# Smaller loads, a split last group on a mixed tile, late tiles inverted first, and a planner with other prices

## The chip, the cores and the metric

The kernel runs on one core of a Trainium2 chip. Its engines are TensorE (PE, with PEld for its weight loads), VectorE (DVE), ScalarE (ACT), GpSimd (POOL, which here issues the gathers) and SyncE (SP, which issues all other transfers). 16 DMA engines move data between HBM and the on-chip memory SBUF; matmuls write into PSUM. The metric is the device time of one execution in microseconds (us).

## The reference

Two branches work on the same x (2048 rows of 576) and are mixed by a gate per row.

```python
def _A_ref(x, w_r, w_i):
    X = rfft2(x)
    return irfft2(X * (w_r + 1j * w_i))

def _B_ref(xf, w_q, k1, k2, u, v):            # 32 heads, K = 1, 64 x 64 experts
    q = einsum("nd,dhc->nhc", xf, w_q)         # 2 x 128 per head
    s1, s2 = q[..., :128] @ k1.T, q[..., 128:] @ k2.T
    e = argmax(s1) * 64 + argmax(s2)           # one expert per row and head
    act = gelu(einsum("nd,nhd->nh", xf, u[e]))
    return einsum("nh,nhd->nd", g * act, v[e]) # g: softmax over one candidate

g = sigmoid((x * gate_w).sum(-1))
return g * _A_ref(x) + (1 - g) * _B_ref(x)
```

## The kernel before

The 2048 rows are 16 tiles of 128. Heads come in 8 chunks `c` of 4. Four kinds of work share the engines.

- **Scores** (`load_wq`, `load_x`, `build_m`, `scores`). For each chunk the weights are multiplied with the keys (`build_m`), five slices `i` of the 576 inputs, of 128 rows each; the fifth holds the last 64 inputs twice. Each operand is split into a high and a low part (`mh`, `ml`, and `xts` for x), and `scores` sums 14 matmuls of 512 columns per tile and chunk. DVE finds the maxima, ACT and DVE turn them into an index (`ei`).
- **Gathers** (`group`). For a tile and a chunk POOL issues four indirect DMAs; each brings, for every one of 128 rows, the 1152 numbers of `u` and `v` of its expert (4608 bytes) into a buffer of the ring `uv` (12 buffers, and one more, `uv2`, late). DVE takes the dot product with x (L496, `z`), ACT the gelu (L500, `b`), DVE the product with the softmax weight (L501, `a`). Then the `v` rows are summed, either by DVE in four multiply-adds (L514) or, where `is_d` holds, on PE: ACT makes diagonal matrices (L524, `dg`) and PE adds eight matmuls into PSUM (`pd`), from which the sum is copied (L538) or added (L540). Of the late tiles 10 to 15, the even ones go by PE, over all eight chunks in one PSUM buffer (`sums`).
- **The transform** (`fold`, `unit` with `f2`, `f4`, `f5`, `f6`): forward along the columns, along the rows, product with the filter, and back along the rows, in ten units.
- **Inversion** (`invert`, `mix`): back along the columns for each tile, with the gate as a scale (L830, L831), then one DVE step (L835) that adds (1 - gate) times the gathered sum, and the store.

Tiles 0 to 9 (`E_T`) have their gathers beside the scores. Then the pools are switched (`switch`), and tiles 10 to 15 (`L_SEQ`) have theirs beside the transform and the inversion, in pairs (10, 11), (12, 13), (14, 15), by `SEQ`.

The order on each engine is not written by hand. Every step is entered in a `Plan` with an engine, an expected duration, a due time `at`, what it reads and writes, and the buffers it needs. `Plan.order` plays the steps through and, whenever an engine is free, takes the one with the smallest due time among those that are ready and find a buffer; the order in which they start there is the order in the program, on SP and POOL too. A gather is entered with 1.13 for its issue and 1.65 for its move. Due times of late groups are spaced `TGS` = 6.6 apart and begin `TLAG` = 10 after the end of the scores, `T0`; those of the transform and the inversion are scaled by `FPACE`, a unit being 14 of it. A due time is no start time: work can be ahead of it or behind it.

PSUM is a ring (`p2`) of four buffers of 128 x 2 x 512, which all matmuls share.

Of the kernel before, what the change touches and what calls it, by code (L numbers as in the profile page):

```python
# [32 lines left out]
def _tables():  # L33
# [10 lines left out]
    def rows(fn, ds):  # L44
        return fn(2 * np.pi * np.outer(ds, k) / D)

    z = np.zeros((P, DF))
    ct = z.copy()
# [4 lines left out]
    fwd = np.stack([  # L53
        rows(np.cos, np.arange(0, 128)), rows(np.cos, np.arange(128, 256)), ct,
        -rows(np.sin, np.arange(0, 128)), -rows(np.sin, np.arange(128, 256)), -st,
    ])
    ck = np.full(DF, 2.0)
    ck[0] = ck[-1] = 1.0
    ck /= S * D

    def irows(fn, ks):
        return fn(2 * np.pi * np.outer(ks, k) / D) * ck[ks][:, None]

    ct = z.copy()
    ct[:33] = irows(np.cos, np.arange(256, 289))
    st = z.copy()
    st[64:96] = irows(np.sin, np.arange(256, 288))
    inv = np.stack([
        irows(np.cos, np.arange(0, 128)), irows(np.cos, np.arange(128, 256)), ct,
        irows(np.sin, np.arange(0, 128)), irows(np.sin, np.arange(128, 256)), st,  # L70
# [12 lines left out]
        "t_fi": c(np.concatenate([fwd, inv]).transpose(1, 0, 2)),  # L83
        "t_f4": c(f4),
        "t_f6": c(f6),
# [167 lines left out]
def tile_kernel(ctx, tc, xn, xT, wqT, kT, wri, uv, gw, t_kr, t_fi, t_f4, t_f6, t_io, out):  # L253
# [84 lines left out]
    gate = pp.tile([P, NT], F32, tag="gate", name="gate")  # L338
    gone = pp.tile([P, NT], F32, tag="gone", name="gone")
# [590 lines left out]
```

## Time and profile before

| | |
|---|---|
| median of 3 runs | 1009.44 us (1008.35 to 1010.46) |
| the profiled execution | 1001.24 us, span 999.5 us |
| mean granted clock of TensorE | 0.965 |
| DVE, PE, DMA queues 0 and 1 | 92%, 90%, 80.9% and 12.3% |
| gathers | 512, 302 MB of 348 MB moved |

Lines of the page and of the trace read as engine, line of the kernel, operation, written tile <- read tiles, shapes, count; a bracket gives the idle time of the engine just before and what ended it. L313 is the line of the helper through which all matmuls go, so matmuls are told apart by their tiles. A busy PE is not a PE at its peak, since the ends of matmuls are modelled.

### The profile page before, as it was taken

How to read it: one execution, taken by the hardware profiler on the slowest of the kernel's cores; microseconds unless marked ns; L12 is line 12 of the kernel's file. 1: busy time of each engine (PE TensorE's matmuls, PEld its weight loads, DVE VectorE, ACT ScalarE, POOL GpSimd, SP SyncE). 2: the span in 40 equal slices, each digit the busy share in tenths (PEclk: the TensorE clock that was granted, in tenths of full speed). 3: DMA queues.
4: the chain of work that ended last, by engine and by line, in shares of the span. 5: the costliest groups of instructions: out<-in, count | busy, mean ns of one | idle time of the engine just before them, and what ended most of it. 6: DMA issues, size and time to landing. Idle time of an engine off the chain costs nothing. (4 is left out here: it accounts for less than half of the span.)

```text
span 999.5 us, 14406 instructions
## 1 busy us (share of the span) xinstructions
PE 904.4 (90%) x4208; PEld 735.8 (74%) x4208; DVE 916.7 (92%) x2255; ACT 514.6 (51%) x1877; POOL 574.4 (57%) x516
## 2 busy tenths in 40 slices
PE   8997999999999999999998990777999998899993
PEld 7885888878877888887877880665777776677762
DVE  3996999999999999999999999999999999977776
ACT  3874676676666576676666664522212222233331
POOL 0354656565656565755657566476655565676662
PEclk9997999999999999999999996889999999899998
DMA  9987999998989999998999799889999999999994
GB/s 336 336 286 301 349 361 367 358 352 305 392 309 361 371 344 332 395 345 328 386 360 330 291 394 378 340 312 389 394 357 351 357 353 321 349 390 414 398 359 192
DMA packets 93246, 348.39 MB, mean 349 GB/s; under 512 B 10480, under 2 KB 13296, under 8 KB 93168
## 3 DMA queue, kind: packets, MB, share of 16 engines
q0 software_dynamic: 73728, 302.02, 80.9%
q1 hardware_dynamic: 19440, 45.45, 12.3%
q8 instruction: 34, 0.56, 0.2%
q14 instruction: 44, 0.36, 0.1%
HBM read 342.71 MB, written 4.72 MB: 348 GB/s over the span
## 5 line engine op out<-in xcount | busy, mean ns | idle before, releaser
L487 POOL DMA_INDIRECT uv<-uv,ei x512 | 574.2, 1121 | 406.2 <-PE p L313 133.3
L313 PE MATMUL p<-mh,xt 128*128 128x512 f32 x1152 | 383.3, 402 | 9.1 <-ACT sg L435 7.3
L435 ACT ACTIVATE sg<-p,mx 128x64 bf16<-128x64 f32 x1024 | 225.8, 352 | 78.1 <-DVE mx L427 55.7
L514 DVE SCALAR_TENSOR_TENSOR xn<-uv,a,xn 128x576 f32<-128x576 f32 x322 | 262.0, 814 | 1.5
L313 PEld LDWEIGHTS p<-mh,xt 128*128 128x128 f32 x1152 | 218.4, 190 | 59.5 <-ACT sg L435 7.7
L313 PE MATMUL p<-ml,xt 128*128 128x512 f32 x640 | 253.2, 396 | 0.0
L496 DVE SCALAR_TENSOR_TENSOR uv<-uv,xn 128x576 f32<-128x576 f32 x320 | 236.3, 749 | 8.7 <-DMA uv<-uv,ei 6.8
L313 PE MATMUL p<-uv,dg 128*128 128x288 f32 x720 | 194.0, 425 | 29.3 <-ACT dg L524 22.5
L313 PEld LDWEIGHTS p<-uv,dg 128*128 128x128 f32 x720 | 140.8, 199 | 77.9 <-ACT dg L524 29.3
L496 DVE SCALAR_TENSOR_TENSOR uv<-uv,xl 128x576 f32<-128x576 f32 x192 | 141.5, 751 | 0.2
L313 PEld LDWEIGHTS p<-ml,xt 128*128 128x128 f32 x640 | 121.6, 190 | 26.6
L500 ACT ACTIVATE b<-z 128x4 f32<-128x4 f32 x128 | 26.4, 206 | 204.9 <-DVE uv L496 171.4
L313 PE MATMUL p<-fi,bt 128*128 128x289 f32 x384 | 97.7, 408 | 4.4 <-DVE t L710 3.0
L313 PEld LDWEIGHTS p<-fi,bt 128*128 128x128 f32 x384 | 83.5, 242 | 16.5 <-issue 3.7
L313 PEld LDWEIGHTS p<-kT,uv 128*128 128x128 f32 x640 | 77.8, 195 | 7.9 <-issue 4.8
L313 PE MATMUL p<-kT,uv 128*128 128x128 f32 x640 | 78.5, 279 | 5.0 <-DMA uv<-wqT 5.0
L427 DVE TENSOR_REDUCE mx<-p 128x16 f32<-128x1024 f32 x64 | 77.5, 1211 | 3.2 <-PE p L313 3.0
L313 PE MATMUL p<-t,t 128*128 128x289 f32 (+2 forms) x384 | 73.8, 362 | 5.9 <-issue 3.4
L446 ACT ACTIVATE sg<-sg 128x256 bf16<-128x256 bf16 x192 | 72.3, 427 | 1.2
L313 PEld LDWEIGHTS p<-t,t 128*128 128x128 f32 (+1 forms) x384 | 54.1, 165 | 23.9 <-issue 10.7
L524 ACT ACTIVATE dg<-ident,a 128x128 f32<-128x128 f32 x180 | 57.6, 393 | 17.7 <-DVE a L501 14.8
L313 PE MATMUL p<-kr,f 128*128 128x128 f32 x160 | 23.0, 301 | 31.5 <-ACT f L648 26.8
(86 smaller groups left out, 612.1 us busy)
## 6 DMA issues: line engine op xcount, KB each, us to landing
uv<-wqT SPq DMA_DIRECT2D x40, 512.0 KB
uv<-uv,ei POOLq DMA_INDIRECT x512
uv<-xT SPq DMA_DIRECT2D x20, 256.0 KB
w<-wri SPq DMA_DIRECT2D x16, 289.0 KB
out<-xn SPq DMA_DIRECT2D x16, 288.0 KB
xn<-xn SPq DMA_DIRECT2D x10, 288.0 KB
t<-t_f SPq DMA_DIRECT2D x18, 128.0 KB
fi<-t_fi SPq DMA_DIRECT2D x2, 867.0 KB
```

Source lines behind the costliest of these rows:

```text
L313: after("PE", nc.tensor.matmul(*args, **kw))
L427: dv(dve(1024, True), at, lambda: nc.vector.tensor_reduce(mv.ap[:, 2 * tp : 2 * tp + 2, :], ps.ap.rearrange("p a (g e) -> p a g e", e=E), ...
L435: on("ACT", actv(sg.ap[:, j, g, :], ps.ap[:, j, g * E : g * E + E], AF.Sign, bias=mv.ap[:, 2 * tp + j, g : g + 1], scale=-1.0))
L446: ac(act(256), at, lambda b=b: actv(s2()[:, :, b * Q : b * Q + Q], s2()[:, :, b * Q : b * Q + Q], AF.Copy, bias=b / 4), [sg], [])
L487: on("POOL", nc.gpsimd.indirect_dma_start(out=g.ap.rearrange("p a d -> p (a d)"), out_offset=None, in_=uv, in_offset=bass.IndirectOffsetOn ...
L496: dv(0.68, at, lambda k=k, g=rows[k]: stt(g.ap[:, 0, :], g.ap[:, 0, :], 1.0, x.ap, op0=ALU.mult, op1=ALU.mult, accum_out=z.ap[:, k : k + 1 ...
L500: ac(0.18, at - 9, lambda: actv(b.ap, z.ap, AF.Gelu_apprx_tanh), [b], zk, table="gelu")
L514: dv(0.73, at, lambda v=v, s=s: stt(y.ap, v(), s(), y.ap, op0=ALU.mult, op1=ALU.add), [y], [(rows[k], 1), a])
L524: ac(0.3, at - 9, lambda k=k, dg=dg: actv(dg.ap, ident, AF.Copy, scale=a.ap[:, k : k + 1]), [dg], [a, "ident"])
```

## The change

- The fifth slice of x and of the weights is loaded once, with 64 rows or columns, instead of doubled (`x5`, `wq5`); the second half of the high part is made on chip, by a second ACT copy in `build_m`. The low part of the fifth slice has 64 rows in its matmul.
- x for blocks 2 and 3 comes in one load for both.
- The inversion uses the same cosine and sine tables (`fi`) as the forward transform; what differed goes into signs, into the fold (a scale of 2 on one column) and into the gate (`gsc`). The two twiddle tables of a unit come in one load (`tw`).
- The place that the second table held goes to a second late gather buffer (`NG2` = 2).
- Late even tiles keep their gathered sum in PSUM until `mix`, which reads it there and writes into the inverted tile; L538 is not used for them. `mix` and the store (`send`) are entered apart.
- Tiles 10 to 15 are inverted first, tiles 0 to 9 after them (`INV`). `FPACE` is 1.4 instead of 1.7.
- The last group (tile 15, chunk 7) is entered in two pairs of gathers, after the tile has been mixed; (1 - gate) is then part of its weights.
- The planner enters a gather with 1.3 for the issue and 1.55 for the move.

```diff
+    fi = np.stack([
+        c0, rows(np.cos, np.arange(128, 256)), ct,
+        rows(np.sin, np.arange(0, 128)), rows(np.sin, np.arange(128, 256)), st,
     ])
...
+        "t_fi": c(fi.transpose(1, 0, 2)),
+        "t_tw": c(np.concatenate([f4[:, :, ::-1], f6], 2)),
...
-        w = wq_t[c, i] = buf("uv", ROW, view=lambda x: x.rearrange("p a d -> p (a d)")[:, : 8 * P].rearrange("p (g e) -> p g e", g=8))
-        ld(load(P * 4096, 4096), at, lambda: nc.sync.dma_start(w.ap, wqT[c, i]), [w], after=after)
-
-    def load_x(b, i, at, at2):
-        st = buf("uv", ROW, view=lambda x: x[:, 0, :512])
-        ld(load(P * 2048, 2048), at, lambda: nc.sync.dma_start(st.ap, xT[:, i, b * 512 : b * 512 + 512]), [st])
-        hi = xts[i if i < 4 else 8][b]
-        lo, r = (xts[4 + i][b], 0) if i < 4 else (hi, 64)
-        ac(act(512), at2, lambda: actv(hi.ap, st.ap, AF.Copy), [hi], [st])
-        dv(dve(512), at2, lambda: vt(lo.ap[r:], st.ap[r:], hi.ap[r:].bitcast(F32), ALU.subtract), [lo], [st, hi])
+        e = P if i < 4 else E
+        w = wq_t[c, i] = buf("uv", ROW, view=lambda x: x.rearrange("p a d -> p (a d)")[:, : 8 * e].rearrange("p (g e) -> p g e", g=8))
+        ld(load(P * e * 32, e * 32), at, lambda: nc.sync.dma_start(w.ap, wqT[c, i] if i < 4 else wq5[c]), [w], after=after)
+
+    def load_x(b, i, at, at2, n=1):
+        st = buf("uv", ROW, view=lambda x: x.rearrange("p a d -> p (a d)")[:, : n * 512])
+        h = P if i < 4 else E
+        src = lambda: xT[:, i, b * 512 : (b + n) * 512] if i < 4 else x5[:, b * 512 : (b + n) * 512]
+        ld(load(h * n * 2048, n * 2048), at, lambda: nc.sync.dma_start(st.ap[:h], src()), [st])
+        for m in range(n):
+            hi = xts[i if i < 4 else 8][b + m]
+            lo, r = (xts[4 + i][b + m], 0) if i < 4 else (hi, E)
+            cut = lambda m=m: st.ap[:h, m * 512 : m * 512 + 512]
+            ac(act(512), at2, lambda hi=hi, cut=cut: actv(hi.ap[:h], cut(), AF.Copy), [hi], [st])
+            dv(dve(512), at2, lambda hi=hi, lo=lo, cut=cut: vt(lo.ap[r : r + h], cut(), hi.ap[:h].bitcast(F32), ALU.subtract), [lo], [st, hi])
...
+        for r in range(0, P, h):
+            ac(act(512), at, lambda r=r: actv(v3(mh)[r : r + h], pv()[:h, :, :E], AF.Copy), [(mh, r)], [pm])
+        dv(dve(512, True), at, lambda: vt(v3(ml)[:h], pv()[:h, :, :E], v3(mh)[:h].bitcast(F32), ALU.subtract), [(ml, 0)], [pm, (mh, 0)])
...
+            seq = [(x, mh, P), (x, ml, h)] + ([(xts[4 + i][b], mh, P)] if i < 4 else [])
 
             def go():
-                for n, (xx, m) in enumerate(seq):
-                    mm(ps.ap[:, j, :], xx.ap[:, tsl], m.ap, start=i == n == 0, stop=i == 4 and n == len(seq) - 1)
-
-            use = {id(q): q for pair in seq for q in pair}
-            return plan("PE", 0.23 * len(seq), at, go, [(ps, j)], list(use.values()))
+                for n, (xx, m, k) in enumerate(seq):
+                    mm(ps.ap[:, j, :], xx.ap[:k, tsl], m.ap[:k], start=i == n == 0, stop=i == 4 and n == len(seq) - 1)
+
+            use = [x, (ml, 0)] + [(mh, r) for r in range(0, P, h)] + ([xts[4 + i][b]] if i < 4 else [])
+            return plan("PE", 0.23 * len(seq), at, go, [(ps, j)], use)
...
-    def group(t, c, at, ahead, gate_by=()):
-        rows = []
-        for k in range(HPC):
+    def group(t, c, at, ahead, gate_by=(), ks=range(HPC), mixed=False):
+        rows = {}
+        for k in ks:
...
-            plan("POOL", 1.13, at - ahead, go, [(g, 0), (g, 1)], [("ei", t // 2, c)], move=1.65, after=gate_by)
-            rows.append(g)
+            plan("POOL", 1.3, at - ahead, go, [(g, 0), (g, 1)], [("ei", t // 2, c)], move=1.55, after=gate_by)
+            rows[k] = g
...
+        part_of = lambda: gone[:, t : t + 1] if mixed else 1.0
+        dv(0.08, at, lambda: stt(a.ap[:, k0:k1], b.ap[:, k0:k1], part_of(), sw[:, t, c * HPC + k0 : c * HPC + k1], op0=ALU.mult, op1=ALU.mult),
+           [a], [b, ("sw", t, c)] + ["gone"] * mixed)
...
-        last = c == NCH - 1
-        if part or t not in sums:
-            sums[t] = psum()
-        pd = sums[t]
+        last = not any(is_d(t, n) for n in range(c + 1, NCH))
+        if part:
+            pd = psum()
+        elif t in sums:
+            pd = sums[t]
+        else:
+            pd = sums[t] = psum()
...
-        if part or last:
+        if last and not part:
+            accs[t] = pd
+        elif part or last:
...
-        load_x(2, i, 15, 24)
+        load_x(2, i, 15, 24, 2)
...
-    for i in range(ND):
-        load_x(3, i, 34, when(3))
...
-            ("t2", "ip", NT2), ("bt", "ip", 1), ("fi1", "ip", 1), ("krb", "ip", 1),
+            ("t2", "ip", NT2), ("bt", "ip", 1), ("fi", "ip", 1), ("krb", "ip", 1),
             ("uv2", "x2", NG2), ("xl", "x2", NT - NE), ("gr", "x2", 1),
-            ("f5", "fp", 2), ("kr", "fp", 1), ("fi0", "fp", 1), ("t4", "fp", 2), ("t6", "fp", 2), ("w", "fp", 2)):
+            ("f5", "fp", 2), ("kr", "fp", 1), ("tw", "fp", 2), ("w", "fp", 2)):
...
-    ld(load(P * 6936, 4096), T0 + 90, lambda: nc.sync.dma_start(fi[1].ap, t_fi[:, 6:12, :]), [fi[1]])
...
+        tw = tabs[k] = buf("tw", [P, 8, P])
+        ld(load(P * 2048, 2048), at - 8, lambda: nc.sync.dma_start(tw.ap[:, 1:5, :], t_tw[k]), [(tw, 0)])
...
+        dv(0.1, at, lambda: nc.vector.tensor_scalar(gsc, gate, 2.0 / (S * D), None, op0=ALU.mult), ["gsc"], ["gate"])
...
+        if t in sums:
+            accs[t] = ga
+            half = lambda x: x.rearrange("p (r d) -> p r d", r=2)
+            dv(0.77, at, lambda: stt(half(ga.ap), y.ap[:, :, :288], gone[:, t : t + 1], half(ga.ap), op0=ALU.mult, op1=ALU.add),
+               [(ga, 0), (ga, 1), ga], [y, "gone"])
+            return
         dv(0.73, at, lambda: stt(y.ap, y.ap, gone[:, t : t + 1], ga.ap, op0=ALU.mult, op1=ALU.add), [y], [(ga, 0), (ga, 1), "gone"])
+
+    def send(t, at):
+        y = accs[t]
...
-    for n, t in enumerate(E_T + L_SEQ):
+    for n, t in enumerate(INV):
         at = inv0 + FPACE * 4.2 * n
         invert(t, at)
         if t in E_T:
             mix(t, at + 5)
+            send(t, at + 5)
...
+    held = score_jobs[NCH - 1, 7][:1]
     for n, (t, c) in enumerate(SEQ):
-        group(t, c, TR + TGS * n, AHEAD, score_jobs[NCH - 1, 7][:1])
-        if c == NCH - 1:
-            mix(t, TR + TGS * n + 9)
+        at = TR + TGS * n
+        if c < NCH - 1:
+            group(t, c, at, AHEAD, held)
+        elif n < len(SEQ) - 2:
+            group(t, c, at, AHEAD, held)
+            mix(t, at + 9)
+            send(t, at + 9)
+        elif t % 2 == 0:
+            group(t, c, at, AHEAD, held)
+            mix(t, at + 9)
+            send(t, at + 9)
+        else:
+            mix(t, at - 4)
+            for ks in LAST:
+                group(t, c, at + 1.65 * ks[0], AHEAD, held, ks, True)
+            send(t, at + 9)
...
-NG2 = 1
+NG2 = 2
...
-FPACE = 1.7
+FPACE = 1.4
...
+INV = L_SEQ + E_T
+LAST = (0, 1), (2, 3)
```

More of the change, by code (lines that the diff above doesn't have):

```diff
@@ L47, in _tables @@
     z = np.zeros((P, DF))
+    c0 = rows(np.cos, np.arange(0, 128))
+    c0[0] *= 0.5
     ct = z.copy()
@@ L252, in tile_kernel @@
 @with_exitstack
-def tile_kernel(ctx, tc, xn, xT, wqT, kT, wri, uv, gw, t_kr, t_fi, t_f4, t_f6, t_io, out):
+def tile_kernel(ctx, tc, xn, xT, x5, wqT, wq5, kT, wri, uv, gw, t_kr, t_fi, t_tw, t_io, out):
     nc = tc.nc
@@ L507, in group @@
             y = accs[t]
-            for k in range(HPC):
+            for k in ks:
                 v = lambda k=k: rows[k].ap[:, 1, :]
```

120 lines of the change are left out of this document (47 added, 73 removed).

## The prediction

> **What bounds the kernel now.** I read the page first (busy shares, then the DMA queues), then busy time by stage, the waits, and the timeline of the last 30 us.
>
> ```profile
> span 999.5 us, 14406 instructions
> PE 904.4 (90%) x4208; PEld 735.8 (74%) x4208; DVE 916.7 (92%) x2255; ACT 514.6 (51%) x1877; POOL 574.4 (57%) x516
> q0 software_dynamic: 73728, 302.02, 80.9%
> q1 hardware_dynamic: 19440, 45.45, 12.3%
> ```
>
> Three resources stand near 90%: TensorE, VectorE (DVE) and the DMA engines (80.9 + 12.3 = 93% for the two big queues). An average hides which one limits when, so next the same by stage; the columns are window, length, busy us of PE, PEld, DVE, ACT and POOL, granted clock, DMA share, GB/s.
>
> ```profile
> 0.00:36.00 36.00, 31.04 (x176) 27.42 (x177) 17.79 (x34) 19.14 (x49) 0.20 (x4) 1.00 0.95 344
> 36.00:100.00 64.00, 56.48 (x265) 46.15 (x263) 54.23 (x141) 41.53 (x159) 33.52 (x32) 0.92 0.83 298
> 100.00:605.00 505.00, 492.06 (x2331) 403.04 (x2329) 494.13 (x1241) 335.99 (x1303) 308.73 (x273) 0.99 0.94 351
> 605.00:862.00 257.00, 204.93 (x960) 167.56 (x960) 249.35 (x608) 75.47 (x255) 153.31 (x138) 0.91 0.96 356
> 862.00:981.00 119.00, 114.07 (x464) 87.54 (x464) 90.66 (x215) 40.27 (x107) 78.59 (x71) 1.00 1.00 385
> 981.00:999.50 18.50, 5.84 (x16) 4.04 (x16) 10.57 (x22) 2.23 (x7) 0.00 (x0) 0.78 0.30 114
> ...
> DVE uv L496 <- DMA uv<-uv,ei: 5.4, 8, 1.2
> ...
> POOL uv L487 <- PE p L313: 42.0, 18, 5.2
> ...
> POOL uv L487 <- DVE xn L514: 25.5, 18, 4.9
> ```
>
> From 100 to 605 (scores, with the gathers of tiles 0 to 9) DVE is busy 494.1 of 505 us, 98%, and it waited for gathered rows only 5.4 us in that window (first wait row): DVE bounds this stage. From 605 to 862 (the transform beside the gathers of the late tiles) DVE is at 97% and DMA at 0.96: both. The last two rows, of this window, say why a gather is late there: its buffer has not been released. From 862 to 981 (inversion) DMA is at 1.00 and PE at 114 of 119, while DVE has 28 us to spare: the gathers pace it. The last 18.5 us have almost nothing on the DMA engines: a tail of dependent steps.
>
> **The tail, step by step.**
>
> ```profile
> 971.13 2.22 PE L313 MATMUL p<-t,krb 128*128 128x289 f32 x8 [0.74 <-ACT t L819]
> ...
> 975.12 4.15 PE L313 MATMUL p<-uv,dg 128*128 128x288 f32 x16 [1.77 <-ACT dg L524]
> ...
> 979.74 1.10 POOL L487 DMA_INDIRECT uv<-uv,ei  x1 [0.30 <-issue]
> ...
> 984.64 5.84 PE L313 MATMUL p<-uv,dg 128*128 128x288 f32 x16 [5.38 <-ACT dg L524]
> ...
> 986.19 0.76 DVE L496 SCALAR_TENSOR_TENSOR uv<-uv,xl 128x576 f32<-128x576 f32 x1
> ...
> 990.51 0.65 ACT L538 ACTIVATE xn<-p 128x576 f32<-128x576 f32 x1 [5.05 <-PE p L313]
> 991.06 0.20 ACT L500 ACTIVATE b<-z 128x4 f32<-128x4 f32 x1
> 991.19 0.82 DVE L835 SCALAR_TENSOR_TENSOR xn<-xn,gone,xl 128x576 f32<-128x576 f32 x1 [4.24 <-ACT xn L538]
> 991.93 0.16 DVE L501 SCALAR_TENSOR_TENSOR a<-b,sw 128x4 f32<-128x4 f32 x1
> 992.12 3.38 DVE L514 SCALAR_TENSOR_TENSOR xn<-uv,a,xn 128x576 f32<-128x576 f32 x4
> 995.54 0.82 DVE L835 SCALAR_TENSOR_TENSOR xn<-xn,gone,xl 128x576 f32<-128x576 f32 x1
> ```
>
> Tile 15's last dot product ends at 986.95 (986.19 + 0.76), but its gelu (L500) stands in ACT's queue behind tile 14's copy out of PSUM (L538), and that waits for PE until 990.5. Then come tile 14's mix, four multiply-adds, tile 15's mix (996.36), and the store until 999.5, 3.14 us. After the change L538 is gone, tile 15's mix is done before its last group, and only two multiply-adds follow the last pair. Tile 15: 986.95 + 0.20 (gelu) + 0.16 + half of 3.38 + some 0.4 of hand-overs + 3.14 = 992.5. Tile 14: PE ends at 990.48, its mix reads PSUM (about 0.8, priced below), store: 990.48 + 0.1 + 0.8 + 3.14 = 994.5. The later counts: the tail shrinks by 999.5 - 994.5 = 5.0 us. With the 16 matmuls at 4.15 us, as the row at 975 has them, tile 14 would end at 992.8, and the gain is 6.7. I take 5.0, because the inversions of the first ten tiles now stand in PE's queue here and may cost what their warmth brings.
> The slow 16 matmuls came after 5.38 us without PE work. The Trainium skill, "TensorE: Matmul & The Clock Gate", Part 1, says PE falls to half its clock after an idle window of some 3.4 us and is released after as long a busy one; by that rule a PE kept busy by the inversions would give the 6.7, by the row as it stands 5.0.
>
> **Loads.**
>
> ```profile
> uv<-wqT SPq DMA_DIRECT2D x40, 512.0 KB
> ...
> uv<-xT SPq DMA_DIRECT2D x20, 256.0 KB
> ...
> fi<-t_fi SPq DMA_DIRECT2D x2, 867.0 KB
> ```
>
> Queue q1 moved 45.45 MB in 12.3% of 999.5 us: 2.70 us per MB; q0 gives 808.6 / 302.02 = 2.68. Both prices agree though their packets differ in size, so I charge bytes alone, and merging each pair of twiddle tables (same bytes) counts zero. Eight of the 40 weight loads halve: 2.10 MB. Four of the 20 x loads halve: 0.52 MB. One of the two 867 KB tables goes: 0.89 MB. Of DMA time that is 5.7 + 1.4 + 2.4 us. The first two lie mostly where DVE bounds, which waited 5.4 us for rows: worth 0 to 7, I take 2 (the start, at 0.95 DMA, has the x loads). The table lies where DMA is at 0.96 to 1.00: 0 to 2.4, I take 2. Sum of the loads: 4.
>
> **One more gather buffer.** 14 instead of 13 after the switch. Between 605 and 862 gathers waited 42.0 + 25.5 us for buffers, and DMA idled 4% of 257 = 10 us. So 0 to 10; one part in 13 of 67.5 us is 5, the half of it hidden because DVE is full: 2.
>
> **What costs nothing, and under which cover.**
>
> ```profile
> L487 POOL DMA_INDIRECT uv<-uv,ei x512 | 574.2, 1121 | 406.2 <-PE p L313 133.3 <-issue 105.6 <-DVE xn L514 55.4
> ...
> L313 PE MATMUL p<-kT,uv 128*128 128x128 f32 x640 | 78.5, 279 | 5.0 <-DMA uv<-wqT 5.0
> ...
> L396 ACT ACTIVATE mh<-p 128x512 fp32r<-128x512 f32 x40 | 24.5, 613 | 19.4 <-remote 9.2 <-PE p L313 7.7 <-issue 2.5
> ...
> L540 DVE TENSOR_TENSOR xn<-p,xn 128x576 f32<-128x576 f32 x18 | 13.5, 751 | 1.6 <-PE p L313 1.5
> ...
> L313 PE MATMUL p<-t,t 128*33 128x128 f32 x128 | 10.2, 279 | 0.0
> ```
>
> Eight more ACT copies of the halved chunk: 8 x 0.613 = 4.9 us, hidden since ACT is busy 336 of 505; without cover 0 to 4.9. What queues behind each are the sign operations that release PSUM. Matmuls that use part of the array: 33 columns and 128 columns both take 279 ns, so the 64-row contractions change nothing. DVE reading PSUM takes 751 ns (L540) against 0.82 for L835: a mix from PSUM costs no more. The factor moved into the gate is one DVE instruction of 16 columns. Sign flips keep counts. The stores of tiles 0 to 9 move behind the late tiles' in SP's queue, 0.295 MB or 0.8 us each; nothing but stores stands there by then.
> The planner's prices only change the order: 1.3 for an issue (1.121 plus the 0.30 gap before it is 1.42) and 1.55 for a move (80.9% of 999.5 over 512 is 1.58). Both come nearer or stay about as near. Order cannot raise a DVE at 98%, and it can open holes; I take 0, with a bound of about one hole each way:
>
> ```profile
> 88.50 0.79 PE L313 MATMUL p<-mh,xt 128*128 128x512 f32 x1 [7.28 <-ACT sg L435]
> ```
>
> ```profile
> 769.22 6.02 PE L313 MATMUL p<-fi,bt 128*128 128x289 f32 x24
> ...
> 779.49 0.75 DVE L753 TENSOR_TENSOR t<-p,t 128x578 f32<-128x578 f32 x1
> ...
> 769.42 0.65 ACT L538 ACTIVATE xn<-p 128x576 f32<-128x576 f32 x1 [3.36 <-PE p L313]
> ...
> 779.72 0.58 ACT L766 ACTIVATE f<-p 128x512 f32<-128x512 f32 x1
> ...
> 841.99 0.60 ACT L766 ACTIVATE f<-p 128x512 f32<-128x512 f32 x1 [0.58 <-PE p L313]
> ...
> 867.14 0.65 ACT L819 ACTIVATE t<-p 128x578 f32<-128x578 f32 x1
> ...
> 883.51 0.65 ACT L538 ACTIVATE xn<-p 128x576 f32<-128x576 f32 x1 [3.14 <-PE p L313]
> ```
>
> The transform's pace, 1.7 to 1.4, only moves due times, by which the planner picks among ready steps. Taking 605 as the switch, tile 10's last group was due 10 + 14 x 6.6 = 102 us after it and its sum left PSUM at 769 (769.42, L538), 164 after: gathers' work runs some 60 us overdue. The back half of unit 7 was due at 1.7 x (20.8 + 112) + 12 = 238, and its copy (L766) came at 842, 237 after: on time. At 1.4 it is due at 198, 40 earlier, so the groups keep the first claim on DVE and the transform stays what fills it up. I take 0. If it did overtake, DMA would idle before 862, and every percent of its share lost over those 257 us comes back as 2.6 us behind.
>
> **Sum:** -5 (tail) -4 (loads) -2 (buffer) = -11. The profiled execution took 1001.24 us (span 999.5 and 1.7 around it), so 990.2 for its like; the median of the runs, 1009.44, stands 8.2 above it, and from there the forecast is 998.4 us.
>
> **Rivals.**
>
> *PSUM is held too long (slower).* Before, L538 empties tile 10's sum at 769.4 and tile 12's at 883.5. Now a sum keeps one of four PSUM buffers until its tile is inverted, and the first inversion comes at 867. So from 769 on tiles 10 and 12 hold two, and the transform has two where it had three. It makes a unit in (841.99 - 779.72) / 3 = 20.8 us; one product pair occupies a buffer from 769.2 to 780.2. If its pace goes with the buffers, a unit takes 31.1: 10.4 more, for the four units after 769, so 0 to 42 us. The last inversion's PE work ended at 973.4; two scalings, mix and store add 5, so the chain ends at 978 + d, behind nothing until d is about 16, and slower than before from d = 21. At d = 30 the span is 1008.4, +9: 1018. For it: PE is full from 862 on and cannot catch up. Against it: DVE, not PSUM, is at 97% there, due times of the transform shrink from 1.7 to 1.4, and inverting late tiles first frees the sums soonest. The Trainium skill, "PSUM — Partial Sum Buffer", Summary: rules for kernel authors, tells to "evacuate promptly", which speaks against this edit; no row here prices it.
>
> *The new order closes the early holes (faster still).* Between 36 and 100 DMA stands at 0.83, and PE lost 7.28 us in one wait. If prices nearer to the traced ones and x loads two blocks at a time close that, 8 to 12 us more go: 988. Against it: the hole came from queue order on ACT, which the prices of gathers do not touch.
>
> *Everything is hidden (no change).* If the new order opens one hole of the same size, 7 to 11 us, it eats the 11: 1006 to 1010.
>
> **How the numbers follow.** Forecast 0.45 (993 to 1004); early holes closed 0.2 (985 to 993); hidden 0.08 (1006 to 1011); PSUM 0.27 (1011 to 1030). Range 985 to 1019: it leaves out the upper part of the PSUM case and a little below. A measurement of this kernel tells 0.2%, 2 us, from no change. Faster 0.66; same 0.05; slower 0.29.
>
> **What would show it.** Right: no L538-like copy for tiles 10, 12 and 14; last gather to end of span under 15 us (now 19.8); DMA near 1.00 from the switch to the last gather; first inversion no later than 870. Wrong: PE waiting on PSUM releases between 770 and the first inversion, the first inversion after 885, or stores of tiles 0 to 9 as the last thing on the chip; or DVE below 96% between 100 and 605.

## The result, and the profile after

The changed kernel took 1062.45 us (median of 4 runs, 1059.26 to 1065.88) where the kernel before took 1008.89 (4 runs, 1006.11 to 1010.46): a ratio of 1.0535 [1.0488, 1.0581]. It is 5% slower; the forecast was 1% faster, 998.4 us, and its range ended at 1019. The profiles show one execution each, with spans of 1062.9 and 999.5 us: they lie 63 us apart where the medians lie 54, so differences read between the two can be some 10 us too large in all. First the page's span, engines, two big queues and chain.

```profile
span 1062.9 us, 14340 instructions
...
PE 968.9 (91%) x4208; PEld 735.3 (69%) x4208; DVE 920.6 (87%) x2257; ACT 516.5 (49%) x1883; POOL 594.5 (56%) x516
...
q0 software_dynamic: 73728, 302.02, 77.2%
q1 hardware_dynamic: 17088, 41.94, 10.7%
...
PE 57%; DVE 21%; DMA 10%; issue 7%; POOL 2%; ACT 2%; SPq 0%; another core or an unknown queue 0%; ACTq 0%; POOLq 0%; DVEq 0%
```

PE executes as many instructions as before (4208) and is busy 64.5 us longer; DVE gained 4. The loads are smaller as planned (45.45 MB fell to 41.94), so the loss is not there. Busy time by stage, with the columns of the prediction's table; the scores end at about 650 now, not 605.

```profile
36.00:100.00 64.00, 62.52 (x278) 46.25 (x277) 57.66 (x150) 45.05 (x169) 38.48 (x31) 1.00 0.78 285
100.00:650.00 550.00, 538.64 (x2325) 398.69 (x2324) 497.96 (x1238) 336.54 (x1303) 327.45 (x274) 0.98 0.88 319
650.00:1062.90 412.90, 336.77 (x1442) 264.85 (x1442) 348.42 (x842) 116.72 (x367) 228.41 (x209) 0.92 0.89 337
```

In the middle row PE has 2325 records, before 2331 in 505 us: the same work, 45 us longer. PE is at 98% and DVE fell from 98% to 91%, so PE now bounds this stage. Granted clock (0.98, before 0.99) and idle time do not explain it: PE's busy time itself grew from 492 to 539 us, so the matmuls must have spread. The groups by shape show where; the part after the bar is the idle time before them.

```profile
L299 PEld LDWEIGHTS p<-ml,xt 64*128 64x128 f32 x128 | 23.4, 183 | 44.7 <-issue 44.7
L299 PE MATMUL p<-ml,xt 64*128 64x512 f32 x128 | 63.6, 497 | 0.8 <-issue 0.8
L299 PE MATMUL p<-ml,xt 128*128 128x512 f32 x512 | 201.2, 393 | 0.9 <-issue 0.9
```

Half the contraction rows take longer, 497 ns against 393, and before each of their weight loads stand 0.35 us of "issue" (44.7 over 128). The timeline of one such place:

```profile
307.23 0.42 PEld L299 LDWEIGHTS p<-mh,xt 128*128 128x128 f32 x2
...
307.46 0.63 PE L299 MATMUL p<-mh,xt 128*128 128x512 f32 x2
...
308.02 0.18 PEld L299 LDWEIGHTS p<-ml,xt 64*128 64x128 f32 x1 [0.37 <-issue]
...
308.45 0.19 PEld L299 LDWEIGHTS p<-mh,xt 128*128 128x128 f32 x1 [0.25 <-issue]
...
308.45 0.50 PE L299 MATMUL p<-mh,xt 128*128 128x512 f32 x1
...
308.79 0.39 PE L299 MATMUL p<-ml,xt 128*128 128x512 f32 x1
...
309.02 0.64 PE L299 MATMUL p<-mh,xt 128*128 128x512 f32 x2
```

Among matmuls of 128 rows one starts every 0.23 us (308.79, 309.02), and the next weights load beside the running matmul. Before the 64-row load PEld stands still for 0.37 us, and before the following 128-row load for 0.25; the matmul at 308.45 is followed only 0.34 us later. From 307.46 five matmuls (two in that row, the 64-row one, and those at 308.45 and 308.79) should take 5 x 0.23 = 1.15; the next one starts at 309.02, 1.56 later. So some 0.4 us are lost each time, and 128 x 0.4 = 51 us of TensorE's time.

The change also brings in 128 matmuls of 64 columns, where the weights of the fifth slice are multiplied with the keys. They stand in 8 groups of 16, so the shape changes there only 8 times and back, and their loads have 1.0 us of idle time before them in all: too little to matter here.

```profile
L299 PEld LDWEIGHTS p<-kT,uv 128*64 128x64 f32 x128 | 13.8, 137 | 1.0
```

After the switch another 19 us went: from the transform's first fold (ACT, L647, at 672.4; before at 628.4) to the end of the span are 390.5 us against 371.1. The end:

```profile
1028.64 1.61 POOL L482 DMA_INDIRECT uv<-uv,ei  x1 [0.52 <-issue]
...
1039.64 1.67 DVE L511 SCALAR_TENSOR_TENSOR xn<-uv,a,xn 128x576 f32<-128x576 f32 x2
...
1042.35 4.04 PE L299 MATMUL p<-uv,dg 128*128 128x288 f32 x16
1046.23 2.11 PE L299 MATMUL p<-t,krb 128*128 128x289 f32 x8
1046.43 0.82 DVE L836 SCALAR_TENSOR_TENSOR xl<-p,gone,xl 128x576 f32<-128x576 f32 x1 [4.39 <-PE p L299]
1048.18 6.01 PE L299 MATMUL p<-fi,bt 128*128 128x289 f32 x24
1054.03 4.06 PE L299 MATMUL p<-t,krb 128*128 128x289 f32 x16
```

Tile 15's last two multiply-adds end at 1041.3 and tile 14 is mixed from PSUM (L836) at 1047.3; both are done. But PE still inverts tiles until 1058.1. The last gather was issued 34.3 us before the end (before: 19.8), and from 1025 to 1050 the DMA share is down to 0.48 while PE is full:

```profile
1025.00:1050.00 25.00, 25.00 (x104) 19.45 (x103) 17.31 (x35) 7.15 (x19) 2.54 (x2) 1.00 0.48 186
```

So the gathers do not pace the end any more; the inversion on PE does.

### The profile page after: what moved, and what is told of

Same layout as the page of the kernel before. It is cut to its first block, busy times and chain, and to the rows that moved or that the text cites. A ratio compares the mean times of both kernels' runs of the same rounds, so it can differ in the third digit from the quotient of the medians.

```text
span 1062.9 us, 14340 instructions
## 1 busy us (share of the span) xinstructions
PE 968.9 (91%) x4208; PEld 735.3 (69%) x4208; DVE 920.6 (87%) x2257; ACT 516.5 (49%) x1883; POOL 594.5 (56%) x516
## 3 DMA queue, kind: packets, MB, share of 16 engines
q1 hardware_dynamic: 17088, 41.94, 10.7%
## 4 chain that ended last, share of the span: by engine, by line
PE 57%; DVE 21%; DMA 10%; issue 7%; POOL 2%; ACT 2%; SPq 0%; another core or an unknown queue 0%; ACTq 0%; POOLq 0%; DVEq 0%
PE p L299 57%; DMA uv<-uv,ei 8%; DVE uv L492 7%; DVE xn L511 6%; POOL uv L482 2%; DVE mx L422 1%; DVE sg L443 1%; DMA uv<-wq 1%; DVE t L706 1%; DVE bt L772 1%; DMA uv<-xT 1%; DVE t L707 1%; ACT dg L524 0%; DMA xn<-xn 0%; DVE im L446 0%
## 5 line engine op out<-in xcount | busy, mean ns | idle before, releaser
L482 POOL DMA_INDIRECT uv<-uv,ei x512 | 594.3, 1161 | 435.5 <-PE p L299 173.7
L299 PE MATMUL p<-mh,xt 128*128 128x512 f32 x1152 | 390.0, 408 | 1.9 <-issue 1.0
L299 PE MATMUL p<-ml,xt 128*128 128x512 f32 (+1 forms) x640 | 264.8, 414 | 1.8 <-issue 1.8
L299 PE MATMUL p<-uv,dg 128*128 128x288 f32 x720 | 202.7, 439 | 28.3 <-ACT dg L524 18.9
L299 PEld LDWEIGHTS p<-uv,dg 128*128 128x128 f32 x720 | 147.0, 207 | 77.8 <-ACT dg L524 23.0
L299 PEld LDWEIGHTS p<-ml,xt 128*128 128x128 f32 (+1 forms) x640 | 119.9, 187 | 63.1 <-issue 45.2
L299 PE MATMUL p<-kT,uv 128*128 128x128 f32 (+1 forms) x640 | 82.1, 284 | 5.1 <-DMA uv<-wqT 5.1
L299 PEld LDWEIGHTS p<-kT,uv 128*128 128x128 f32 (+1 forms) x640 | 75.3, 184 | 13.0 <-issue 10.9
L390 ACT ACTIVATE mh<-p 128x512 fp32r<-128x512 f32 (+1 forms) x48 | 29.0, 603 | 74.6 <-PE p L299 66.4
L299 PE MATMUL p<-tw,t 128*128 128x256 f32 (+1 forms) x256 | 43.9, 353 | 11.2 <-DVE t L708 5.1
```

The lines of the kernel that those rows point to most:

```text
L299: after("PE", nc.tensor.matmul(*args, **kw))
L390: ac(act(512), at, lambda r=r: actv(v3(mh)[r : r + h], pv()[:h, :, :E], AF.Copy), [(mh, r)], [pm])
L482: on("POOL", nc.gpsimd.indirect_dma_start(out=g.ap.rearrange("p a d -> p (a d)"), out_offset=None, in_=uv, in_offset=bass.IndirectOffsetOn ...
```

## The experiments

The chips of the experiments ran the kernel before in 990 to 999 us, so each ratio is to its runs on the same chip. "Fold" is the start of the first fold (20 to 27 us after the last matmul of the scores), "d" the time from it to the first inversion's second step (`p<-t,krb`), "tail" the time from the last gather's issue to the end of the span; all are read from the timelines of one execution each, in us. They are not scaled: the chip of after ran the kernel before in 1008.89 us, so after's own row stands some 2% high beside the others.

| kernel | ratio, 95% interval | fold | d | tail |
|---|---|---|---|---|
| before (again, e8) | 0.9986 [0.9965, 1.0007] | 622.7 | 240.9 | 19.6 |
| after | 1.0535 [1.0488, 1.0581] | 672.4 | 287.2 | 34.3 |
| e1 after, 128 rows, order kept | 1.0425 [1.0359, 1.0491] | 653.0 | 276.6 | 34.3 |
| e2 before, 64 rows | 1.0338 [1.0302, 1.0374] | 656.6 | 244.9 | 20.0 |
| e3 before, 64 rows in pairs | 1.0100 [1.0066, 1.0135] | 630.0 | 241.7 | 19.5 |
| e4 after, low part on 128 rows | 1.0240 [1.0200, 1.0280] | 627.2 | 273.8 | 34.3 |
| e5 = e4, sums copied out | 1.0057 [1.0032, 1.0082] | 631.6 | 261.8 | 28.1 |
| e6 = e1 with the old prices | 1.0214 [1.0172, 1.0257] | 639.1 | 259.7 | 22.5 |
| e7 = e4, pace 1.7 | 1.0395 [1.0363, 1.0428] | 633.5 | 299.9 | 60.6 |
| e9 after, old prices | 1.0371 [1.0336, 1.0407] | 657.0 | 260.9 | 22.5 |
| e10 late half, pace 1.2 | 0.9969 [0.9943, 0.9995] | 614.6 | 234.2 | 19.1 |
| e11 = e5, pace 1.1 | 1.0223 [1.0183, 1.0263] | 631.3 | 235.6 | 18.3 |
| e12 before, last group split | 0.9974 [0.9950, 0.9998] | 621.5 | 240.4 | 19.1 |
| e13 before, both new prices | 1.0327 [1.0259, 1.0395] | 657.7 | 260.8 | 29.9 |
| e14 = e10, pace 1.4 | 1.0025 [0.9997, 1.0053] | 627.0 | 254.0 | 23.6 |
| e15 = e14, one sum held | 1.0030 [0.9996, 1.0064] | 625.1 | 254.3 | 23.6 |
| e16 = e14, all sums held | 1.0040 [1.0002, 1.0078] | 627.6 | 262.2 | 22.7 |
| e17 before, issue price 1.3 | 1.0057 [1.0032, 1.0083] | 629.5 | 241.3 | 19.5 |
| e18 before, move price 1.55 | 1.0378 [1.0345, 1.0411] | 656.3 | 261.9 | 29.9 |

### The matmuls of 64 rows

**e1**, the order of after left as it is; this matmul reads the high part of the weights of the last 64 inputs a second time, so their low part is left out and the high part counts twice.

```diff
-            seq = [(x, mh, P), (x, ml, h)] + ([(xts[4 + i][b], mh, P)] if i < 4 else [])
+            seq = [(x, mh, P), (x, ml if i < 4 else mh, P)] + ([(xts[4 + i][b], mh, P)] if i < 4 else [])
```

> The changed kernel, with its order on every engine untouched; only the 64-row matmul of the fifth slice is replaced by a 128-row one (it reads the high part again instead of the low part, so the low part of 64 of 576 inputs is left out of the scores). Theory 1, TensorE pays for each of the 128 matmuls that use 64 rows between ones that use 128: the trace of the changed kernel shows 44.7 us idle before their weight loads and 497 ns for one against 393, so 45 to 55 us go and the time is 1008 to 1018 us. Theory 2, the new order of the work (prices, due times, PSUM held longer) costs the time and the rows are innocent: 1057 to 1066 us.

It came between the two theories: 1.1% of the 5.35 went, and the fold still came at 653. Row count is one cause, and there is another in the same order. Waits of PE from 100 to 600, first of after, then of e1:

```profile
PE p L299 <- ACT b L496: 7.8, 5, 2.1
```

```profile
PE p L299 <- DVE a L498: 28.1, 6, 5.2
```

Of what PE gains with 128 rows, e1 spends some 20 us waiting for gathered groups (`a`, the weights of their sums).

**e2**, the kernel before with this one matmul on 64 rows, nothing else (the product of the two low parts of the last 64 inputs is left out).

```diff
+                    k = E if i == 4 and m is ml else P
-                    mm(ps.ap[:, j, :], xx.ap[:, tsl], m.ap, start=i == n == 0, stop=i == 4 and n == len(seq) - 1)
+                    mm(ps.ap[:, j, :], xx.ap[:k, tsl], m.ap[:k], start=i == n == 0, stop=i == 4 and n == len(seq) - 1)
```

> The kernel before, same order on every engine; only the low-part matmul of the fifth slice contracts 64 rows instead of 128 (the product of the two low parts of these 64 inputs is left out). Theory 1: PE had some 13 us to spare between 100 and 605, so 30 to 50 us are added, 1039 to 1059 us. Theory 2: nothing, 1007 to 1011 us.

+3.4%, 33 us, from one operand cut in half. That is near what the lost time says: 51 us on a PE that had 505 - 492 = 13 us to spare in that stage leaves 38. Its groups by shape are those of after:

```profile
L313 PEld LDWEIGHTS p<-ml,xt 64*128 64x128 f32 x128 | 23.4, 183 | 44.5 <-issue 42.7 <-DVE xn L515 1.1 <-DVE xn L541 0.4
L313 PE MATMUL p<-ml,xt 64*128 64x512 f32 x128 | 63.8, 499 | 0.0
```

**e3**, the same 128 matmuls, but those of a pair of tiles one behind the other.

```diff
+                if i == 4:
+                    mm(ps.ap[:, j, :], x.ap[:, tsl], mh.ap, start=False, stop=False)
+                    for o in (1, 0) if j == 1 else ():
...
+                        mm(ps.ap[:, o, :], x.ap[:E, usl], ml.ap[:E], start=False, stop=True)
+                    return
```

> The kernel before with the 64-row matmuls of the two tiles of a step put next to each other: as many of them, but half the changes between 64 and 128 rows. If the price is per change of the row count, half of what the unpaired version adds, 1022 to 1035 us; if it is per matmul of 64 rows, the same, 1039 to 1059 us; theory 2: 1007 to 1012 us.

```profile
L313 PEld LDWEIGHTS p<-ml,xt 64*128 64x128 f32 x128 | 18.9, 185 | 23.1 <-issue 21.3 <-DVE xn L521 1.4 <-DVE uv L503 0.4
L313 PE MATMUL p<-ml,xt 64*128 64x512 f32 x128 | 46.6, 444 | 0.0
```

As many 64-row matmuls, half the changes of row count, and the idle time before their loads halves (44.5 to 23.1). One such pair:

```profile
312.30 0.86 PE L313 MATMUL p<-mh,xt 128*128 128x512 f32 x3
313.09 0.73 PE L313 MATMUL p<-ml,xt 64*128 64x512 f32 x2
313.74 0.50 PE L313 MATMUL p<-mh,xt 128*128 128x512 f32 x1
314.08 0.40 PE L313 MATMUL p<-ml,xt 128*128 128x512 f32 x1
314.32 0.62 PE L313 MATMUL p<-mh,xt 128*128 128x512 f32 x2
```

Seven matmuls from 312.30 to 314.32 take 2.02 us where 7 x 0.23 would be 1.61: a pair loses the same 0.4 us as a single one. So the price belongs to the change between 128 and 64 rows, not to the 64 rows. The time falls to less than half, from 3.4% to 1.0%, since 64 x 0.4 = 26 us is paid from the same 13 to spare. The Trainium skill, "TensorEngine Tiling (Array Packing)", Key Properties, has a rule for the tile modes of the array: "Mode switching requires drain: Changing tiling mode (not just tile) drains the TensorE". The page does not say that a plain matmul of 64 rows is such a switch; the traces look as if it were, with 0.4 us for going to 64 rows and back. The same skill's "TensorE: Matmul & The Clock Gate", Part 2, says that a weight load's time goes by its columns, not by the contraction rows; the loads agree (183 and 188 ns), and it is the spacing that rises.

**e4**, after with the low part made for both halves by a second DVE step, so that all matmuls have 128 rows (a new order comes with it).

```diff
-            seq = [(x, mh, P), (x, ml, h)] + ([(xts[4 + i][b], mh, P)] if i < 4 else [])
+            seq = [(x, mh, P), (x, ml, P)] + ([(xts[4 + i][b], mh, P)] if i < 4 else [])
...
-        dv(dve(512, True), at, lambda: vt(v3(ml)[:h], pv()[:h, :, :E], v3(mh)[:h].bitcast(F32), ALU.subtract), [(ml, 0)], [pm, (mh, 0)])
+        for r in range(0, P, h):
+            dv(dve(512, True), at, lambda r=r: vt(v3(ml)[r : r + h], pv()[:h, :, :E], v3(mh)[:h].bitcast(F32), ALU.subtract), [(ml, r)], [pm, (mh, 0)])
```

> The changed kernel with the low part of the fifth slice made twice (a second DVE subtraction, 8 more of 0.68 us) and all matmuls of the scores over 128 rows; the planner orders anew. Theory 1: 1008 to 1022 us. Theory 2: 1057 to 1070 us. Below 1005 only if the rest of the change brings the 11 us that the prediction summed.

The fold is back at 627 (622.7 in e8), and the ratio at 1.024, between the two theories again: nearly all of the loss in the scores is gone, and what is left lies mostly behind the switch (d 273.8, tail 34.3). The profile is of the quickest of four executions, 1004.52 us against a median of 1012.47. e1 and e4 differ by 1.85% with the same matmul shapes; between them lies the order.

### The planner's prices

**e9**, after with the prices of before; **e6**, the same two lines in e1.

```diff
-            plan("POOL", 1.3, at - ahead, go, [(g, 0), (g, 1)], [("ei", t // 2, c)], move=1.55, after=gate_by)
+            plan("POOL", 1.13, at - ahead, go, [(g, 0), (g, 1)], [("ei", t // 2, c)], move=1.65, after=gate_by)
```

> The changed kernel with nothing undone but the planner's prices of a gather (1.13 and 1.65 again). The 64-row matmuls and the held sums stay, so some 30 us and some 18 us over the kernel before stay too. If the new prices cost by themselves what the pair of 128-row versions says (ratio 1.0425 against 1.0214), the ratio falls from 1.0535 to 1.03 to 1.04; if that was the luck of one order, it stays at 1.045 to 1.06.

> The changed kernel with the 64-row matmul replaced by a 128-row one that reads the high part again (the low part of 64 inputs left out, as in the first experiment), and the planner's prices of a gather back at 1.13 and 1.65. In the first experiment, with the new prices, the scores still took 25 us more than before, and DVE waited 25.8 us for gathered rows between 100 and 600. If the shorter move price is the cause, those waits fall below 10 us, the first fold comes before 635 us and the ratio to the kernel before is 1.00 to 1.03. If not, the fold stays at 645 to 660 and the ratio at 1.035 to 1.05.

The old prices take 1.6% off after and 2.1% off e1. From e1 to e6 the fold comes 14 us earlier and d falls from 277 to 260. After was run on a slower chip; scaled to e9's (1.0535 x 990.77 over its own 1064.66, a factor of 0.98) it has its fold at 659 and a d of 282, against 657 and 261 in e9, so there nearly all of the gain is in d. The prices are not the whole of the loss by order: e6 lies between its two expectations, its fold is still 16 us behind that of e8 on the same chip, and DVE still waits 18.7 us for rows there, 17.9 in e9.

**e13**, the kernel before with both new prices; **e17**, with 1.3 alone; **e18**, with 1.55 alone.

> The kernel before with the planner's prices of a gather at 1.3 and 1.55 and nothing else. Putting the old prices back into the changed kernel took 1.6% off it, with the first fold 15 us earlier and the transform 26 us earlier. If the prices do that by themselves, this is 1.01 to 1.025, with the fold or the first inversion later by 10 us or more; if they only hurt beside 64-row matmuls, which the planner does not price, 0.995 to 1.005.

> The kernel before with the price of issuing a gather at 1.3 instead of 1.13, the move still 1.65. Both prices together cost 3.3%, with DVE waiting 27 us for gathered rows and PE 28 us for weights of such groups between 100 and 600. In the plan moves of 1.65 follow one another more slowly than issues of 1.3, so the issue price should change little: ratio 0.995 to 1.008, DVE waits for rows below 12 us. If it is the issue price that does it, 1.02 to 1.035.

> The kernel before with the price of moving a gather at 1.55 instead of 1.65, the issue still 1.13. A gather took 1.58 us of the DMA engines: if a move priced below that lets the planner set consumers ahead of their rows, ratio 1.02 to 1.035 and 20 us or more of DVE waits for rows between 100 and 600; if any other order does as well, 0.995 to 1.008.

The issue's price is worth 0.6%, the move's 3.8%: one number in a planner's table, and the same work in another order. Busy time from 100 to 600, first of before, then of e18.

```profile
100.00:600.00 500.00, 490.21 (x2324) 401.90 (x2323) 489.13 (x1229) 333.80 (x1295) 305.56 (x269) 0.99 0.94 351
```

```profile
100.00:600.00 500.00, 467.13 (x2172) 381.52 (x2171) 458.66 (x1149) 311.71 (x1208) 280.90 (x249) 0.97 0.90 326
```

In e18 every engine and the DMA do less in the same 500 us, and none is full. Waits of DVE and PE in that stage of e18 (us in total, times, longest):

```profile
DVE uv L496 <- DMA uv<-uv,ei: 29.8, 32, 2.7
...
PE p L313 <- ACT b L500: 22.1, 6, 5.6
PE p L313 <- ACT dg L524: 10.7, 6, 3.0
DVE xn L540 <- PE p L313: 9.0, 6, 2.5
```

DVE waits 29.8 us for rows; before it was 5.4, in e8 7.0 and in e17 6.6. The gathers take 1.58 us of the DMA engines each (the prediction's figure). A likely reading: with 1.65 the planner reckons with rows a little later than they come; with 1.55, a little earlier, and it places the dot product ahead of them. A dot product whose rows are late then holds everything that the program has behind it on DVE, and PE waits in turn for the gelu and the diagonal matrices of that group. The waits fit this; the planner's own clock is in no trace. The price that costs 3.8% is 2% below the measured one, and that of the kernel before 4% above it. No other price was tried, so it is not shown that being below is what costs, and not this one order.

### Sums held in PSUM, and the pace

**e5**, e4 with the sums of tiles 10, 12 and 14 copied out of PSUM as before.

```diff
-        if last and not part:
-            accs[t] = pd
-        elif part or last:
+        if part or last:
...
-        if t in sums:
+        if False:
```

> The changed kernel with all score matmuls over 128 rows, and the sums of tiles 10, 12 and 14 copied out of PSUM when their last group is done, as before (ACT copy, mix from SBUF); the rest of the change stays. Theory 1b, the held sums slow the transform: in the 128-row version the first inversion's second step came 274 us after the first fold, against 244 in the kernel before, and the inversions of the early tiles were the last thing; with the copies that distance falls to 240 to 255 us, and the time to 15 to 25 us below the version that holds, 0.985 to 1.00 of the kernel before. Theory 2b, the due times (pace 1.4, late tiles first) slow it: the distance stays near 274 and the ratio near 1.024.

1.0240 falls to 1.0057: holding the sums costs 1.8% here. But d falls only to 262, not to the 240 to 255 expected, so the hold is a part of its growth. Beside e8 on the same chip, e5 has its fold 9 us later and takes 1 us less from there to the end (366.1 against 367.4). The Trainium skill, "PSUM — Partial Sum Buffer", Summary: rules for kernel authors, with its "evacuate promptly" has this run on its side; e16 below shows where the hold costs nothing that can be measured.

**e7**, e4 with `FPACE` 1.7, and **e11**, e5 with `FPACE` 1.1.

> The changed kernel with all score matmuls over 128 rows and the transform's pace back at 1.7; PSUM is held as in the change. If the pace is of no account (groups stay overdue and go first), the ratio is that of pace 1.4, 1.015 to 1.033. If 1.4 helps the transform through its shortage of PSUM, 1.7 is slower, 1.03 to 1.06; if 1.4 takes DVE from the gathers, 1.7 is faster, 0.99 to 1.01.

> The version with 128-row matmuls and copied sums, pace 1.1 instead of 1.4. There the gathers ended 338 us after the first fold, 10 earlier than before, but the transform was 21 us late and the inversions ended last. If the pace moves work from gathers to the transform: first inversion's second step 240 to 255 us after the fold (262 at 1.4), ratio 0.99 to 1.00. If the groups keep the first claim whatever the pace: 258 to 265 and 1.003 to 1.009.

The pace moves work. From 1.4 to 1.7 d rises from 274 to 300 and the tail to 60.6; from 1.4 to 1.1 d falls from 262 to 236, and the last gather comes 360.7 us after the fold, not 338.0. Either way the time rises by 1.6%: the one delays the inversion, the other the gathers. In e11 d falls even below the 240 to 255 expected, and the time rises instead of falling.

**e14** has the scores, loads and prices of before and the late half of the change (shared tables, merged twiddles, second late buffer, late tiles inverted first, split last group), sums copied out, `FPACE` 1.4. **e15** is e14 with only tile 14's sum held, **e16** with all three.

```diff
+        if last and t == NT - 2:
+            accs[t] = pd
+        elif part or last:
```

> The version with the scores and prices of before, copied sums and the late half of the change, pace 1.4 instead of 1.2. At 1.2 PE's last inversion ended 330 us after the first fold and the last gather was issued at 348. The pair 1.4 and 1.1 showed that pace moves one against the other, some 8 us for 0.1. So transform later by 10 to 20 us, gathers earlier by 8 to 15, ratio 0.982 to 0.994; if the pace does nothing with these prices, 0.994 to 1.000.

> As the version at pace 1.4 with copied sums, but tile 14 alone is mixed straight from PSUM: its sum is held only after the transform is over. The copy (0.65 us) and the wait of the last gelu behind it go: 1 to 4 us less than the version that copies all three. If the held sum slows the inversions, equal or up to 5 us more.

> As the version at pace 1.4 with copied sums, but all three sums stay in PSUM until the mix, as in the change. Beside the 128-row version that cost 1.8%. If it is the hold itself, first inversion's second step 10 to 25 us later than with the copies, and a ratio 0.01 to 0.025 above. If it only hurt with the new prices, within 0.005.

Three times the same within their intervals, and neither gain came: e14 was expected below 1.000, and e15 1 to 4 us below e14. In e15, as in e14, tile 15's last dot product (L484) stands on DVE behind tile 14's mix (L830), which waits for PE; one such place in e15:

```profile
993.73 0.82 DVE L830 SCALAR_TENSOR_TENSOR xl<-p,gone,xl 128x576 f32<-128x576 f32 x1 [2.49 <-PE p L299]
994.47 0.75 DVE L484 SCALAR_TENSOR_TENSOR uv<-uv,xl 128x576 f32<-128x576 f32 x1
```

Holding all three moves the inversions: d is 8 us longer, and PE's last `p<-t,krb` ends 373.5 us after the fold, not 357.4. Busy time from 985 on, first of e14, where PE has only tile 14's 16 matmuls left, then of e16, where it still inverts:

```profile
985.00:1010.00 25.00, 6.25 (x16) 4.34 (x16) 11.62 (x26) 2.99 (x10) 0.00 (x0) 0.77 0.12 48
```

```profile
985.00:1010.00 25.00, 16.12 (x67) 12.21 (x65) 16.07 (x35) 5.85 (x16) 0.85 (x1) 0.90 0.32 117
```

So the hold delays PE's inversions by some 16 us. In e14 they end 5 us after the last gather is issued (357.4 and 352.3 after the fold), with the steps of tiles 14 and 15 still to come, and the time hardly moves. In e5 they end 23 us after it even without the hold (361.3 and 338.0), and there the hold adds 1.8%. That this difference is the reason is argued from these three kernels, not tested by itself.

### The tail, and the best version

**e12**, the kernel before with only the last group split and tile 15 mixed first (tile 14 still copied out).

```diff
+            mix(t, at - 4)
+            for ks in LAST:
+                group(t, c, at + 1.65 * ks[0], AHEAD, held, ks, True)
+            send(t, at + 9)
```

> The kernel before with the last group of tile 15 in two pairs on a tile that is mixed first, and nothing else; tile 14 is still copied out of PSUM. The prediction's tail: tile 15's path falls to 992.5 of 999.5, tile 14's to 990.5 + 0.65 + 0.8 + 3.1 = 995.1, so 4 to 7 us less, ratio 0.993 to 0.996. If the tail is hidden behind something else, 0.998 to 1.002.

```profile
974.42 7.02 PE L313 MATMUL p<-uv,dg 128*128 128x288 f32 x16 [6.10 <-ACT dg L529]
...
978.58 0.08 DVE L497 DVE_READ_ACCUMULATOR uv<-uv,xl 128x1 f32 x1
...
981.48 0.65 ACT L543 ACTIVATE xn<-p 128x576 f32<-128x576 f32 x1 [6.01 <-PE p L313]
982.03 0.20 ACT L501 ACTIVATE b<-z 128x2 f32<-128x2 f32 x1
982.17 0.82 DVE L840 SCALAR_TENSOR_TENSOR xn<-xn,gone,xl 128x576 f32<-128x576 f32 x1 [3.50 <-ACT xn L543]
983.15 1.67 DVE L516 SCALAR_TENSOR_TENSOR xn<-uv,a,xn 128x576 f32<-128x576 f32 x2
```

The split is worth at most a little: 0.26%, 2.6 us, by the ratio, where the kernel before against itself (e8) came out at 0.14%, and the tail falls only from 19.6 to 19.1 us. Tile 14's 16 matmuls took 7.02 us after 6.10 us without PE work (5.72 after 5.38 in e8), and tile 15's gelu (L501), whose last dot product was done at 978.7 (L497), still stands behind tile 14's copy (L543), so its last two multiply-adds (L516) come after both.

**e10**, e14 with `FPACE` 1.2, was to bring together what had not cost anything.

> The late half of the change on the scores of before: loads, splits and matmuls of the scores and the prices as before; shared tables, merged twiddles, second late buffer, late tiles first, split last group as in the change; sums copied out of PSUM; pace 1.2. If the 64 rows, the held sums and the order of the scores are all that went wrong, the first fold comes as before (620 to 630 us), the transform within 250 us of it, and the ratio is 0.985 to 0.997. If the inversions of the early tiles still end last, 0.997 to 1.01.

0.9969 [0.9943, 0.9995] over 10 runs: some 3 us below the kernel before, the best version with the late half. But its interval overlaps those of e12 (0.9974) and of e8 (0.9986 [0.9965, 1.0007]), so what of this is a gain is not shown.

**e8**, the kernel before once more as a kernel of its own, shows what a comparison can tell.

> The kernel before, for a profile on this chip: ratio 0.995 to 1.005, first inversion's second step 240 to 250 us after the first fold.

## Why the prediction was wrong, by its own steps

**"The 64-row contractions change nothing."** This is the first step that failed. It argued from 33 columns taking as long as 128, but columns are not the contraction rows; the trace of before had no 64-row matmul, and the term got no bound. Alone it measured 33 us (e2), from 0.4 us of PE lost at each of 128 changes to 64 rows and back. Little of it was hidden because PE stood at 492 of 505 us in the prediction's own table: "DVE bounds this stage" was read from 98% against PE's 97%, and a term that fell on PE had 13 us of cover.

**"Order cannot raise a DVE at 98%, and it can open holes; I take 0".** The second. Both clauses hold, but the bound of one hole, 7.28 us, was far off: the holes opened are many and small (32 waits on rows, 2.7 us the longest), and the prices cost 33 to 37 us on the kernel before (e13, e18). "Both come nearer" was taken as harmless; the move's price went from above the measured 1.58 to below it, which may be the side that counts.

**The two do not add.** Alone 3.4% and 3.3 to 3.8%, together with everything else 5.35%. A PE slowed by the changes of row count waits less for the gathered groups: between 100 and 600 it waits 7.8 us for their gelu in after, 28.1 us for their weights in e1. And e4 and e5 have the new prices but little early loss (fold at 627 and 632, against 622.7 in e8; DVE waits 7.9 and 8.9 us). So a price that is too low is a risk that the order of that kernel takes or not. Why e1 took it and e4 not, with one DVE step between them, isn't settled.

**Rival 1, PSUM held too long,** came true as far as it went, and its formula did well: the end of PE's chain at 978 + d. Here the first inversion came 43 us later against the fold, and the fold 44 later: 978 + 87 = 1065, and the span is 1062.9. But the hold is only a part of it: 12 us of d in e5, 8 in e16. The new prices are some 20 of it: 17 from e6 to e1, 21 from e9 to after at one scale, and 21 in e18, which holds no sum. The listed sign, PE waiting on PSUM, is not in the waits; PE's largest wait from 770 to 960 is for diagonal matrices:

```profile
PE p L299 <- ACT dg L524: 13.0, 5, 5.2
```

The planner plays the four buffers through; that it had put the transform later in the order, so that nothing was left to wait for on the chip, is likely, and not shown.

**"The groups keep the first claim"** (pace, costed at zero) failed: e7, e5 and e11 move d by 26 us for each 0.3 of `FPACE`. Why d in e14 (254 at 1.4) is still longer than in the kernel before (241 at 1.7) isn't settled; the second gather buffer is one candidate, and was not tried alone.

**Loads** held in bytes: 3.51 MB less, which is the prediction's 2.10 + 0.52 + 0.89. No run isolates their time; in e5, where the first cause is gone, the last gather comes 338 us after the fold (348 in e8), but by then PE's inversions end last, and from the fold to the end only 1 us is gained. **The buffer** has no run of its own either.

**The tail** was mis-sized: -5.0 forecast, -2.6 at most in e12, where tile 14's copy remains, and nothing more in e15, where that copy is gone and the wait for PE stands in DVE's queue. Its "PE kept busy by the inversions" was right in after (the 16 matmuls take 4.04 us at 1042.35), and useless, because those inversions were what ended last.

**The early hole** of 7.28 us did close: PE is busy 62.5 of the 64 us from 36 to 100. But it belonged to the one execution of the profile: in e8, the same kernel, PE's longest wait there is 1.9 us, and PE is busy 61.8. So it was no gain to be had, and no measure of what an order can open.

Of the signs listed, the missing copy of tiles 10, 12 and 14 held; last gather to end under 15 us (34.3), DMA near 1.00 to the last gather (0.95 from 650 on) and the first inversion by 870 (959.6) did not; DVE below 96% from 100 on was the sign that named the loss. Of the other signs of being wrong, the late first inversion and the early tiles' stores at the very end came too, and PE waiting on PSUM did not.

Along one chain of edits the 5.35% reads: 1.1 for the row count with the order kept (e1), 1.85 for the order (e4), 1.8 for the held sums (e5), and 0.57 left. Each link holds for this chain alone, since each edit but e1's also makes the planner order anew.

## What to carry to other kernels

A bound engine at 98% beside another at 97% is two bounds: cost every edit on both, and give an operation that the trace does not show (here, another row count in the array) a price from both sides, not zero. In an order written by a planner, changing one duration by 6%, to a value just below the measured one, cost 3.8% with the same work to do, and hardly shows in another order (e4): run such a change by itself. Holding a resource longer cost nothing measurable where its user would end 5 us after the last gather (e14 and e16), and 1.8% where it would end 23 us after it (e5 and e4); find that point first.

## What the runs showed of the hardware that was not expected

- A change between 128 and 64 contraction rows delays TensorE: 0.37 us before the 64-row weight load and 0.25 before the next 128-row one, and the matmuls come some 0.4 us late in all (307.46 to 309.02 in after); two 64-row matmuls in a row pay it once (e3).
- TensorE coming back from 6.10 us of idleness took 7.02 us for 16 matmuls, at a granted clock of 0.58, that take 4.15 after 1.77, at 1.00 (e12); before, 5.38 us gave 5.84, at 0.71. The idle time alone does not set it: in e10 the same matmuls took 7.13 us after 3.17. The Trainium skill's "TensorE: Matmul & The Clock Gate", Part 1, has the half clock after an idle window; its direction agrees.
